# Four transposing transfers in place of TensorE transposes for one batch's residual, in an attention-and-mixing kernel

## The chip, the cores and the metric

The kernel runs on one core of one Trainium2 chip. The core has five engines that each work through their own instructions in order: TensorE (PE, matrix products; its weight loads are shown apart as PEld), VectorE (DVE), ScalarE (ACT), GpSimd (POOL) and SyncE (SP). SyncE computes nothing here: it issues transfers (DMAs), which sixteen transfer engines then carry out between the chip's memory and the core's own, or within the core's own. Engines wait for each other on semaphores. The metric is the device time of one execution in microseconds; a smaller time is better. Small differences are told by the median of several runs.

## The reference, cut to what matters

Eight batches, eight heads, 576 positions, 64 channels a head. An attention over means of four positions and an attention over a narrow band (positions less than 4 apart) are added; the result, 576 x 512 a batch, is x. A second stage mixes it:

```python
theta = x @ w_theta
zr, zi = x * cos(theta), x * sin(theta)
y = einsum('ts,bsd->btd', w_tok_r, zr) + einsum('ts,bsd->btd', w_tok_i, zi)
u = x + y
out = u + maximum(u @ w_ch, 0.0)
```

The change concerns the last line: u is needed twice, once as an operand of the product with w_ch (channels on the partitions) and once as the residual that is added to it (positions on the partitions). One of the two is a transpose of the other.

## The kernel before, in words

The work is cut into small steps, each a function with a two-letter name, called with a batch b and a number. One long hand-written list, ORDER, says in which order the steps are emitted. The loop at the end reads it word by word: the first two letters name the step, what follows names its place (a bank of the accumulator memory, a slot of the staging memory, or the engine: v, a, g for VectorE, ScalarE, GpSimd). The b and the number are not in the word; they come from the step's own list in STEPS, in turn. `pin()` chains every instruction to the one before on the same engine, so each engine, SyncE too, runs exactly in the order of ORDER. Semaphore waits between engines are put in by the framework where data or buffers demand them. Batches overlap: while one batch is mixed, the next two or three are loaded, turned and run through attention.

The steps that matter here, for one batch:

- **Loads.** `lk`, `lq` (L287, four each) bring k and q into one of 16 staging slots, 288 KB each; `lv`, `lw` (L347, five each) bring v, 128 KB each. `ck`, `cq` (L295) cast k and q to bfloat16 on the engine named, `cv` (L396) does so for v. SyncE issues the loads in the order of the list, ahead of their use.
- **Attention.** `tp` (L302) transposes k or q on TensorE, for half of the heads at a time; `ev` (L315) brings the result back. For batch 7 `dk` (L306) does so by transposing transfers instead, and `ev` copies at L312. `kd`, `qd` (L329 to L335, or one VectorE instruction) take the means of four, `sd` (L426) the coarse scores, `nd`, `xn` their use; `ps` (L482), `ex`, `mk` (L503, L505), `po` (L515), `nm` (L523, L524) are the banded attention, `xt` (L537) turns its result, and `xa` (L545) adds the coarse one, which gives x with channels on the partitions (tile xT).
- **Mixing.** `th` (L556), `cs` (L561, L562), `xm` (L595) and `zz` make z; the last 64 positions go through `tt`, `ct`, `zt` (L577) and, from batch 4, `dz` (L581), a transposing transfer that writes row block 8 of z. `mx(b, i)` (L636) is nine matmuls that sum over the row blocks 0 to 8 of z in turn, eight such groups a batch; `ua(b, i)` (L641, VectorE) adds xT and writes 288 positions of 128 channels of uT. Two steps, ua(b, 2c) and ua(b, 2c+1), complete channel block c.
- **Residual.** ur[b % 2] holds u with positions on the partitions. For the batches in RPE, `up(b, c)` (L650) makes four TensorE transposes of 128 x 128 into a bank and `uc(b, c)` (L653) copies them out, once for each 128 positions. For the other batches `du(b, c)` (L645) is one transposing transfer issued by SyncE, 128 channels x 512 positions, once for each 128 channels; it needs ua(b, 2c) and ua(b, 2c+1).
- **Output.** `ch(b, c)` (L666) is the product with w_ch for 128 positions, `rl(b, c)` (L674, VectorE) clips it and adds ur, `st` (L680) stores it. The last 64 positions of two batches go together: `ut`, `dt` (L695), `ht` (L700), `rt` (L704), `ss`, `sr` (L709).

RPE is (0, 1, 2, 3): batches 0 to 3 use up and uc, 4 to 7 use du. In the list, the eight steps of batch 3 stand in lines 86 to 88: up(3,0) and up(3,1) after rl(2,3), then uc(3,0) on VectorE and uc(3,1) on ScalarE, up(3,2) and uc(3,2) on ScalarE after mx(4,2), up(3,3) before ch(3,0) and uc(3,3) on ScalarE after rl(3,1). The steps ua(3,0) to ua(3,7), on which they depend, stand in lines 81 to 85, among the loads of batches 6 and 7 and the attention of batches 4 to 6.

Of the kernel before, what the change touches and what calls it, by code (L numbers as in the profile page):

```python
# [44 lines left out]

XDMA = (6, 7)

RPE = (0, 1, 2, 3)
ZPE = (0, 1, 2, 3)

QKD = (7,)
# [26 lines left out]
tp01 eva mx6 mkg xt45 xt23 ua ua cva cvg cvg xt01 cka ts cvg xa xa mx7 th6 xa po45 nm pv23 tt0 th1 lk4 xm4 st st mkg  # L78
th5 vdv st cs nd23 ua zz ct cqg cqg ztg tp67 th4 cs dt po01 cs cs te xn evv po23 mx5 kdg qdg xm4 xm6 mx7 nm ps01 ex nm
ps23 ua lvd ua ex ch5 ps01 ex qdg zz lw lw xm7 zz rl kdg zp6 zz mkg nd23 xn lv1 lva lv3 mx5 zca sd67 lw ps01 ex po34  # L80
mx2 ua lw ed tp01 sd67 cva nm po34 eva cvv cvg ed lw up5 uca ua mx2 cvg nm cvg lvc xd3 ua pv04 xcv lk7 lk0 mx7 lq9 lq6
lq2 lqd lq8 lqb lq5 ckg ckg vda lq7 lw xt56 mkv cqg cqg po34 lk4 xt01 xa xa ch2 st cva ts lv6 th5 up6 ckg xm0 nm th1
tp34 cs ucv cs mkg rl eva mx6 ua ua th1 xt67 lk0 lk1 cs cqa po45 mkv xa nm ht3 rt tp67 th1 eva zz xm2 lv9 xm3 xm4 lw
lve zz zz ckg dk4 kdv mx0 cqg tp67 nd23 xn cs zz ua cqa eva mx1 nd67 xn cqa sr cqa cka tt2 ct dkb up4 cva cva ua mx0
mx7 ua cvg cvv uca te po01 nm qdg kdg qdg sd56 ed po23 ua ch4 rl xd0 ch1 ztg lw nm up7 ch4 uca xca po23 dz xt67 rl evg
ckg nm st st pv15 vda mx0 ps23 xa ex rl up1 up7 evg ua ucv mx6 uca ss ps01 ex xt45 cqa utg xa ua lv1 dk4 ps23 ex mx7
up0 uca th4 lvb sd56 mkv po23 lw lw xt01 utg dt ua dk7 cvv nm th7 du ed ts evg nd56 xa nd23 tt0 xn xn ct qdg mkv mkg
evv mx1 ztg xd2 up0 ua cs ch3 rl cs te mx4 ch7 qdg ps56 rl xcv ua mx1 ex cvg po23 po45 ua uca ps67 ex ht1 nm nm st st
rt cva ss mx0 ua po67 xt45 nm ps23 st xa ex ts du kdg th1 xm0 xm7 cs th6 cs xm4 zz zz zz ch5 rl kdg mx7 ua th0 po67 nm
cs te xt45 xa sd12 ch3 xm0 ch7 ch4 xt56 st ed sd12 mkg mkg ed ts zz dz lw mx0 lv1 du du cvv lw cvg th1 cs rl uta mx3  # L90
st rl rl xa dxb ua po45 po67 pv02 nm nm ua du mx1 vda ch4 dx mkg ua po23 po01 po67 rl sr nm mx5 ua mx4 tt5 dx1 du nm
nm nd23 xn nd01 st mx6 th7 mx2 cs xn xd3 mx0 ua ua xcv ua ua xt67 utv ct dx st st xt45 xt23 xa ch1 rl th0 ch6 ch1 ch7
cs xa xa tt0 zz zz th2 th3 cs st du du ch4 rl zz zz ztg ct dz rl mx2 mx0 mx1 cs ua ua st dxe dx ht0 ua th1 cs th3 dx7
dx zz st st mx2 rl mx1 ua ua cs zz dt mx3 mx1 mx2 zz zz ztg dz mx7 ua mx3 du du du mx6 rt ua ua utg ua st rl du st mx7
mx4 ua ua ua sr mx7 mx6 mx5 ua ua ua du du ua ch7 ch6 ss ch5 rl rl ch7 ch6 ch4 ch3 du du st uta dt sta rl st rl ht7
ch2 sta rl st rl sta rl st rt ssa sr rl sta rm su k0
"""


# [1 line left out]
def kernel(  # L101
# [605 lines left out]
    def tail_store(e):  # L707
        def step(i, w):
            QUEUE.get(w, nc.sync).dma_start(out=out[2 * i + e, 512:576, :], in_=at["ot", i][HALF * e:HALF * e + HALF])  # L709
        return step  # L710
# [3 lines left out]
    def span(*ns):  # L714
        out = [()]
        for n in ns:
            out = [x + (i,) for x in out for i in range(n)]
        return out
# [14 lines left out]
        zp=(zp, [(b,) for b in ZPE]), zc=(zc, [(b,) for b in ZPE]),  # L733
        up=(up, [(b, c) for b in RPE for c in range(4)]), uc=(uc, [(b, c) for b in RPE for c in range(4)]),
        xm=(xm, [(b, c) for b, c in span(B, 4) if b not in XDMA]), dx=(dx, [(b, c) for b, c in span(B, 4) if b in XDMA]), zz=(zz, span(B, 4)), mx=(mx, span(B, 8)),
        ua=(ua, span(B, 8)), du=(du, [(b, c) for b, c in span(B, 4) if b not in RPE]), ut=(ut, span(B)), ch=(ch, span(B, 4)), rl=(rlf, span(B, 4)),
        st=(st, span(B, 4)), rm=(rm, [(B - 1, 3)]), su=(su, [(B - 1, 3)]), dt=(dt, span(4)), ht=(ht, span(4)), rt=(rt, span(4)), ss=(tail_store(0), span(4)), sr=(tail_store(1), span(4)),
# [70 lines left out]
```

## Time and profile before

| What | Value |
|---|---|
| median of three runs | 231.59 us (231.36 to 231.72) |
| profiled execution, whole time | 231.04 us |
| profiled execution, span from first to last instruction | 229.3 us |
| SyncE's transposing transfers ur<-uT | 16, median issue 1224 ns |
| TensorE transposes at L650 | 64, mean 219 ns each |
| copies at L653 | 9 on ScalarE (median 588 ns), 7 on VectorE (416 ns) |
| moved by transfers | 49.41 MB, mean 216 GB/s |

The profile describes one execution. Its page gives each engine's busy time; a line of digits, one for each fortieth of the span, shows the busy tenths. The chain of waits is followed back from the last instruction: each piece is what the next one waited for, so only time in this chain can be saved or lost directly. A timeline lists an engine's instructions in order of time: start, duration, engine, source line, operation, what is written and read, shapes, how many, and in brackets how long the engine had stood idle and what ended that. For SyncE the duration is that of issuing a transfer, not of the transfer itself; the transfer lands some microseconds later. Matmuls overlap in the array, so the mean of one is longer than its share of the time.

### The profile page before, as it was taken

What the parts mean: (1) busy time and instruction counts of PE and PEld (TensorE: products, weight loads), DVE (VectorE), ACT (ScalarE), POOL (GpSimd) and SP (SyncE); (2) the same over time, 40 slices, a digit from 0 to 9 for tenths busy, and PEclk for the clock granted to TensorE, in tenths of its full rate; (3) what the DMA queues carried; (4) which work ended last, traced back from release to release, by engine and by line L of the source; (5) the groups of instructions that cost most, each with busy time, mean ns of one, the idle gap of its engine ahead of it and who ended that gap; (6) DMA issues with size and microseconds to landing.
All of it is one profiled execution on the core that took longest, in us unless ns stands there. A gap on an engine that the chain in (4) does not pass through costs nothing.

```text
span 229.3 us, 9430 instructions
## 1 busy us (share of the span) xinstructions
PE 219.4 (96%) x3970; PEld 152.3 (66%) x3970; DVE 187.8 (82%) x370; ACT 154.3 (67%) x240; POOL 147.4 (64%) x194
## 2 busy tenths in 40 slices
PE   7997899999999999999999999989998999999992
PEld 2475678776878666885785685766655775667741
DVE  6599998989988899889978798798986967648473
ACT  2279999689988999898888997868786132530000
POOL 7589998879996999997978399379933020200000
PEclk9999999999999999999999999999999999999999
DMA  6999987999998799979799996992473466655787
GB/s 180 394 390 390 294 176 212 370 326 174 319 336 162 196 297 265 203 163 284 157 261 353 270 146 175 136 131 77 90 152 84 71 139 186 139 146 132 152 223 268
DMA packets 76795, 49.41 MB, mean 216 GB/s; under 512 B 61136, under 2 KB 61392, under 8 KB 76752
## 3 DMA queue, kind: packets, MB, share of 16 engines
q1 hardware_dynamic: 76096, 47.76, 80.7%
q10 hardware_dynamic: 656, 1.05, 1.3%
q8 instruction: 31, 0.51, 1.0%
q14 instruction: 12, 0.10, 0.2%
HBM read 33.98 MB, written 9.44 MB: 189 GB/s over the span
## 4 chain that ended last, share of the span: by engine, by line
PE 75%; DVE 10%; DMA 5%; POOL 4%; issue 2%; ACT 2%; SPq 0%; DVEq 0%; POOLq 0%; ACTq 0%
PE PS L636 27%; PE PS L666 10%; PE PS L556 10%; PE PS L302 5%; DMA ur<-uT 4%; PE PS L515 2%; PE PS L537 2%; PE PS L595 2%; PE PS L764 2%; PE PS L482 2%; PE PS L568 2%; POOL two L329 1%; POOL pm L503 1%; PE PS L447 1%; DVE pm L505 1%
## 5 line engine op out<-in xcount | busy, mean ns | idle before, releaser
L636 PE MATMUL PS<-WT,z 128*128 128x288 bf16 x576 | 78.1, 286 | 0.0
L636 PEld LDWEIGHTS <-z 128*128 128x128 bf16 x576 | 53.9, 98 | 16.1 <-issue 1.3
L641 DVE TENSOR_TENSOR uT<-PS,xT 128x288 bf16<-128x288 f32 x64 | 28.5, 451 | 10.2 <-PE PS L636 9.4
L561 ACT ACTIVATE cs<-PS,pihc 128x512 bf16<-128x512 f32 x32 | 22.1, 690 | 21.0 <-PE PS L556 13.4
L556 PE MATMUL PS<-wth,xT 128*128 128x512 bf16 x128 | 32.1, 379 | 0.1
L666 PE MATMUL PS<-wch,uT 128*128 128x512 bf16 (+1 forms) x132 | 31.1, 373 | 0.0
L524 DVE TENSOR_TENSOR tmp<-PS,rl 128x512 bf16<-128x512 f32 x40 | 27.6, 691 | 1.4
L545 DVE TENSOR_TENSOR xT<-PS,xdT 128x928 bf16<-128x928 f32 (+1 forms) x24 | 22.3, 952 | 3.7 <-PE PS L537 3.6
L490 ACT ACTIVATE pm<-PS 128x1024 bf16<-128x1024 f32 (+1 forms) x24 | 20.5, 880 | 6.6 <-PE PS L482 5.4
L674 DVE SCALAR_TENSOR_TENSOR osb<-PS,ur 128x512 f32<-128x512 f32 x28 | 19.1, 685 | 6.7 <-DMA ur<-uT 3.9
L577 POOL TENSOR_TENSOR zT<-xT,cst 128x512 bf16<-128x512 bf16 x7 | 10.0, 1422 | 21.8 <-ACT cst L574 21.8
L295 POOL CAST k_tm<-st 128x576 bf16<-128x576 f32 x23 | 15.5, 691 | 7.6 <-DMA st<-in_k_dram 7.5
L770 ACT ACT_TABLE_LOAD x15 | 19.2, 1283 | 0.3
L666 PEld LDWEIGHTS <-uT 128*128 128x128 bf16 x132 | 11.9, 98 | 11.2
L295 POOL CAST q_tm<-st 128x576 bf16<-128x576 f32 x24 | 17.0, 725 | 3.3 <-DMA st<-in_q_dram 3.2
L562 ACT ACTIVATE cs<-PS 128x512 bf16<-128x512 f32 x32 | 19.1, 598 | 0.0
L396 POOL CAST v_w<-st 128x512 bf16<-128x512 f32 x21 | 13.4, 656 | 8.5 <-DMA st<-in_v_dram 8.5
L556 PEld LDWEIGHTS <-xT 128*128 128x128 bf16 x128 | 11.4, 98 | 10.3 <-DVE xT L545 0.7
L503 POOL TENSOR_TENSOR pm<-pm,band 128x512 bf16<-128x512 bf16 x16 | 18.1, 1158 | 0.0
L329 POOL TENSOR_TENSOR two<-qT 128x576 f32<-128x576 bf16 x14 | 16.5, 1177 | 1.5 <-ACT qT L315 1.2
L620 DVE TENSOR_TENSOR z<-PS,cs 128x1024 bf16<-128x1024 bf16 x24 | 15.8, 683 | 0.8 <-issue 0.4
L329 POOL TENSOR_TENSOR two<-kT 128x580 f32<-128x580 bf16 x13 | 15.0, 1154 | 0.4
(123 smaller groups left out, 421.5 us busy)
## 6 DMA issues: line engine op xcount, KB each, us to landing
st<-in_k_dram SPq DMA_DIRECT2D x32, 288.0 KB, 6.2
st<-in_q_dram SPq DMA_DIRECT2D x32, 288.0 KB, 5.8
st<-in_v_dram SPq DMA_DIRECT2D x70, 128.0 KB, 4.9
out_dram<-osb SPq DMA_DIRECT2D x26, 256.0 KB, 3.5
st<-in_v_dram SPq DMA_DIRECT2D x4, 288.0 KB, 3.0
st<-in_moe_w_tok_r_dram SPq DMA_DIRECT2D x4, 288.0 KB, 6.2
st<-in_moe_w_tok_i_dram SPq DMA_DIRECT2D x4, 288.0 KB, 6.0
st<-in_moe_w_theta_dram SPq DMA_DIRECT2D x4, 256.0 KB, 5.9
```

The lines of the kernel that those rows point to most:

```text
L295: COPY[w](out=to, in_=of)
L329: nc.gpsimd.tensor_tensor(out=t, in0=src[:, :, 0:2], in1=src[:, :, 2:4], op=ALU.add)
L490: nc.scalar.activation(out=pm[(3 * b + u) % NPM][:, :, 0:n].rearrange("p e c j w -> p e (c j w)"), in_=at.pop(("ps", b, u))[:, :, 0:4 * W ...
L503: EW[w].tensor_tensor(out=t[:, x], in0=t[:, x], in1=m[:, x], op=ALU.mult)
L524: nc.vector.tensor_tensor(out=tmp[(NCH * b + c) % NTMP].rearrange("p g (j d) -> p g j d", d=D), in0=ps[:, :, :, 0:D], in1=r.unsqueeze(3).t ...
L545: nc.vector.tensor_tensor(out=xT[b % 2][:, :, lo:lo + cnt].rearrange("p e (m j) -> p e m j", j=4), in0=at.pop(("xt", b, u))[:, :, 0:cnt].r ...
L556: nc.tensor.matmul(out=ps, lhsT=xT[b % 2][:, dc, P * c:P * c + P], rhs=wth[:, dc, :], start=(dc == 0), stop=(dc == 3))
L561: nc.scalar.activation(out=t[:, 0, :], in_=ps, func=AF.Sin, bias=pihc, scale=1.0)
L636: nc.tensor.matmul(out=ps, lhsT=z[b % 2][:, j, P * dc:P * dc + P], rhs=WT[:, j, cols], start=(j == 0), stop=(j == 8))
L641: nc.vector.tensor_tensor(out=uT[b % 2][:, dc, cols], in0=at.pop(("mx", b, i)), in1=xT[b % 2][:, dc, cols], op=ALU.add)
L666: nc.tensor.matmul(out=ps[:, cols], lhsT=uT[b % 2][:, dc, P * c:P * c + P], rhs=wch[:, dc, cols], start=(dc == 0), stop=(dc == 3))
L770: nc.scalar.activation(out=idle, in_=pihc, func=TABLE[kind])
```

## The change

Batch 3 leaves RPE. Its eight steps up and uc go out of the list, and four steps du come into it, one after each of ua(3,1), ua(3,3), ua(3,5) and ua(3,7). All other words keep their order, banks and slots. du(3,0) so stands after lv(6,3) and ahead of lk(6,3), lk(7,0) and the loads of q for batches 6 and 7; du(3,1) ahead of lk(7,2) and lk(7,3); du(3,2) between dk(7,0) of q and lw(7,0); du(3,3) ahead of lw(7,0) and dz(4). The functions are not changed. The lines of the list are broken anew, so the diff shows more lines than it alters; cut to those with a change:

```diff
-RPE = (0, 1, 2, 3)
+RPE = (0, 1, 2)
...
-mx2 ua lw ed tp01 sd67 cva nm po34 eva cvv cvg ed lw up5 uca ua mx2 cvg nm cvg lvc xd3 ua pv04 xcv lk7 lk0 mx7 lq9 lq6
+mx2 ua lw ed tp01 sd67 cva nm po34 eva cvv cvg ed lw up5 uca ua mx2 cvg nm cvg lvc xd3 ua du pv04 xcv lk7 lk0 mx7 lq9
...
-tp34 cs ucv cs mkg rl eva mx6 ua ua th1 xt67 lk0 lk1 cs cqa po45 mkv xa nm ht3 rt tp67 th1 eva zz xm2 lv9 xm3 xm4 lw
+th1 tp34 cs ucv cs mkg rl eva mx6 ua ua du th1 xt67 lk0 lk1 cs cqa po45 mkv xa nm ht3 rt tp67 th1 eva zz xm2 lv9 xm3
...
-lve zz zz ckg dk4 kdv mx0 cqg tp67 nd23 xn cs zz ua cqa eva mx1 nd67 xn cqa sr cqa cka tt2 ct dkb up4 cva cva ua mx0
-mx7 ua cvg cvv uca te po01 nm qdg kdg qdg sd56 ed po23 ua ch4 rl xd0 ch1 ztg lw nm up7 ch4 uca xca po23 dz xt67 rl evg
-ckg nm st st pv15 vda mx0 ps23 xa ex rl up1 up7 evg ua ucv mx6 uca ss ps01 ex xt45 cqa utg xa ua lv1 dk4 ps23 ex mx7
-up0 uca th4 lvb sd56 mkv po23 lw lw xt01 utg dt ua dk7 cvv nm th7 du ed ts evg nd56 xa nd23 tt0 xn xn ct qdg mkv mkg
-evv mx1 ztg xd2 up0 ua cs ch3 rl cs te mx4 ch7 qdg ps56 rl xcv ua mx1 ex cvg po23 po45 ua uca ps67 ex ht1 nm nm st st
+xm4 lw lve zz zz ckg dk4 kdv mx0 cqg tp67 nd23 xn cs zz ua cqa eva mx1 nd67 xn cqa sr cqa cka tt2 ct dkb up4 cva cva
+ua du mx0 mx7 ua cvg cvv uca te po01 nm qdg kdg qdg sd56 ed po23 ua du ch4 rl xd0 ch1 ztg lw nm up7 ch4 uca xca po23
+dz xt67 rl evg ckg nm st st pv15 vda mx0 ps23 xa ex rl evg ua mx6 ss ps01 ex xt45 cqa utg xa ua lv1 dk4 ps23 ex mx7
+th4 lvb sd56 mkv po23 lw lw xt01 utg dt ua dk7 cvv nm th7 du ed ts evg nd56 xa nd23 tt0 xn xn ct qdg mkv mkg evv mx1
+ztg xd2 ua cs ch3 rl cs te mx4 ch7 qdg ps56 rl xcv ua mx1 ex cvg po23 po45 ua ps67 ex ht1 nm nm st st rt cva ss mx0 ua
...
```

More of the change, by code (lines that the diff above doesn't have):

```diff
@@ L80 @@
 ps23 ua lvd ua ex ch5 ps01 ex qdg zz lw lw xm7 zz rl kdg zp6 zz mkg nd23 xn lv1 lva lv3 mx5 zca sd67 lw ps01 ex po34
-mx2 ua lw ed tp01 sd67 cva nm po34 eva cvv cvg ed lw up5 uca ua mx2 cvg nm cvg lvc xd3 ua pv04 xcv lk7 lk0 mx7 lq9 lq6
-lq2 lqd lq8 lqb lq5 ckg ckg vda lq7 lw xt56 mkv cqg cqg po34 lk4 xt01 xa xa ch2 st cva ts lv6 th5 up6 ckg xm0 nm th1
-tp34 cs ucv cs mkg rl eva mx6 ua ua th1 xt67 lk0 lk1 cs cqa po45 mkv xa nm ht3 rt tp67 th1 eva zz xm2 lv9 xm3 xm4 lw
-lve zz zz ckg dk4 kdv mx0 cqg tp67 nd23 xn cs zz ua cqa eva mx1 nd67 xn cqa sr cqa cka tt2 ct dkb up4 cva cva ua mx0
@@ L85 @@
-mx7 ua cvg cvv uca te po01 nm qdg kdg qdg sd56 ed po23 ua ch4 rl xd0 ch1 ztg lw nm up7 ch4 uca xca po23 dz xt67 rl evg
-ckg nm st st pv15 vda mx0 ps23 xa ex rl up1 up7 evg ua ucv mx6 uca ss ps01 ex xt45 cqa utg xa ua lv1 dk4 ps23 ex mx7
-up0 uca th4 lvb sd56 mkv po23 lw lw xt01 utg dt ua dk7 cvv nm th7 du ed ts evg nd56 xa nd23 tt0 xn xn ct qdg mkv mkg
-evv mx1 ztg xd2 up0 ua cs ch3 rl cs te mx4 ch7 qdg ps56 rl xcv ua mx1 ex cvg po23 po45 ua uca ps67 ex ht1 nm nm st st
-rt cva ss mx0 ua po67 xt45 nm ps23 st xa ex ts du kdg th1 xm0 xm7 cs th6 cs xm4 zz zz zz ch5 rl kdg mx7 ua th0 po67 nm
@@ L90 @@
[L90 to L94, printed above, removed]
@@ L95 @@
-mx4 ua ua ua sr mx7 mx6 mx5 ua ua ua du du ua ch7 ch6 ss ch5 rl rl ch7 ch6 ch4 ch3 du du st uta dt sta rl st rl ht7
-ch2 sta rl st rl sta rl st rt ssa sr rl sta rm su k0
+mx2 ua lw ed tp01 sd67 cva nm po34 eva cvv cvg ed lw up5 uca ua mx2 cvg nm cvg lvc xd3 ua du pv04 xcv lk7 lk0 mx7 lq9
+lq6 lq2 lqd lq8 lqb lq5 ckg ckg vda lq7 lw xt56 mkv cqg cqg po34 lk4 xt01 xa xa ch2 st cva ts lv6 th5 up6 ckg xm0 nm
+th1 tp34 cs ucv cs mkg rl eva mx6 ua ua du th1 xt67 lk0 lk1 cs cqa po45 mkv xa nm ht3 rt tp67 th1 eva zz xm2 lv9 xm3
@@ new lines @@
+po67 xt45 nm ps23 st xa ex ts du kdg th1 xm0 xm7 cs th6 cs xm4 zz zz zz ch5 rl kdg mx7 ua th0 po67 nm cs te xt45 xa
+sd12 ch3 xm0 ch7 ch4 xt56 st ed sd12 mkg mkg ed ts zz dz lw mx0 lv1 du du cvv lw cvg th1 cs rl uta mx3 st rl rl xa dxb
+ua po45 po67 pv02 nm nm ua du mx1 vda ch4 dx mkg ua po23 po01 po67 rl sr nm mx5 ua mx4 tt5 dx1 du nm nm nd23 xn nd01
+st mx6 th7 mx2 cs xn xd3 mx0 ua ua xcv ua ua xt67 utv ct dx st st xt45 xt23 xa ch1 rl th0 ch6 ch1 ch7 cs xa xa tt0 zz
+zz th2 th3 cs st du du ch4 rl zz zz ztg ct dz rl mx2 mx0 mx1 cs ua ua st dxe dx ht0 ua th1 cs th3 dx7 dx zz st st mx2
@@ L97 @@
+rl mx1 ua ua cs zz dt mx3 mx1 mx2 zz zz ztg dz mx7 ua mx3 du du du mx6 rt ua ua utg ua st rl du st mx7 mx4 ua ua ua sr
+mx7 mx6 mx5 ua ua ua du du ua ch7 ch6 ss ch5 rl rl ch7 ch6 ch4 ch3 du du st uta dt sta rl st rl ht7 ch2 sta rl st rl
+sta rl st rt ssa sr rl sta rm su k0
 """
```

## The prediction

> **What bounds the kernel now.** First the page: the span, the busy shares, the granted clock and the chain that ended last.
>
> ```profile
> span 229.3 us, 9430 instructions
> ...
> PE 219.4 (96%) x3970; PEld 152.3 (66%) x3970; DVE 187.8 (82%) x370; ACT 154.3 (67%) x240; POOL 147.4 (64%) x194
> ...
> PEclk9999999999999999999999999999999999999999
> ...
> GB/s 180 394 390 390 294 176 212 370 326 174 319 336 162 196 297 265 203 163 284 157 261 353 270 146 175 136 131 77 90 152 84 71 139 186 139 146 132 152 223 268
> ...
> PE 75%; DVE 10%; DMA 5%; POOL 4%; issue 2%; ACT 2%; SPq 0%; DVEq 0%; POOLq 0%; ACTq 0%
> ```
>
> TensorE is busy 96% of the span and carries 75% of the chain, at a granted clock of 1.0. Every stage but one is therefore priced in TensorE time, and a TensorE pause is paid in full unless a later wait takes it up. The exception shows when the chain of waits is asked for the stretch after 143 us:
>
> ```profile
> 144.94 0.55 PE PS L650 x8
> ...
> 147.51 1.12 DVE xT L545
> ...
> 148.92 1.75 DVE pm L505
> ...
> 156.67 0.69 DVE osb L674
> ...
> 170.44 4.34 DMA ur<-uT
> ```
>
> From 147.5 to 176 us it runs through VectorE, GpSimd and transfers; after that TensorE takes it again. Two of the four `up` steps that the change removes (L650 x8, 0.55 us) stand in this chain.
>
> Next I read SyncE's timeline, because the four new transfers go into its queue, which holds every load and most stores in program order:
>
> ```profile
> 114.92 2.26 SPq L287 DMA_DIRECT2D st<-in_k_dram  x2
> 117.23 4.17 SPq L287 DMA_DIRECT2D st<-in_q_dram  x8
> ...
> 123.00 0.62 SPq L287 DMA_DIRECT2D st<-in_k_dram  x1
> ...
> 138.41 1.22 SPq L581 DMA_TRANSPOSE z<-zT  x1
> ```
>
> Matched one by one with the words of ORDER, the row at 114.92 is lk(6,3) and lk(7,0) (the 28th and 29th load of k), 117.23 the eight lq of batches 6 and 7, then, left out here, lw(6,3), and 123.00 lk(7,1). The first new word, du(3,0), stands just ahead of lk(6,3), so SyncE will come to it at 114.9 us. It needs both additions of its 128 channels. VectorE's timeline has line 641 eight times a batch; these are the 26th, 28th and 32nd, that is ua(3,1), ua(3,3) and ua(3,7):
>
> ```profile
> 120.34 0.46 DVE L641 TENSOR_TENSOR uT<-PS,xT 128x288 bf16<-128x288 f32 x1 [0.52 <-PE PS L636]
> ...
> 127.81 0.46 DVE L641 TENSOR_TENSOR uT<-PS,xT 128x288 bf16<-128x288 f32 x1 [0.89 <-PE PS L636]
> ...
> 139.81 0.45 DVE L641 TENSOR_TENSOR uT<-PS,xT 128x288 bf16<-128x288 f32 x1
> ```
>
> So SyncE, which runs about 6 us ahead of VectorE here, would stand still from 114.9 until 120.8 with twelve loads behind it. Whether those have time to spare is read on GpSimd, which casts them, and on TensorE, which uses the casts:
>
> ```profile
> 119.79 0.67 POOL L295 CAST k_tm<-st 128x576 bf16<-128x576 f32 x1 [1.46 <-DMA st<-in_k_dram]
> 121.23 1.72 POOL L295 CAST q_tm<-st 128x576 bf16<-128x576 f32 x2 [0.77 <-DMA st<-in_q_dram]
> ...
> 129.63 0.66 POOL L295 CAST k_tm<-st 128x576 bf16<-128x576 f32 x1 [3.84 <-DMA st<-in_k_dram]
> 130.24 0.67 POOL L295 CAST q_tm<-st 128x576 bf16<-128x576 f32 x1
> ...
> 136.61 0.67 POOL L335 TENSOR_TENSOR qd<-two 128x288 bf16<-128x288 f32 x1
> ```
>
> ```profile
> 126.00 0.67 PE L302 MATMUL PS<-ident,q_tm 128*128 128x128 bf16 x9
> ...
> 132.96 0.67 PE L302 MATMUL PS<-ident,q_tm 128*128 128x128 bf16 x9
> ...
> 138.73 0.36 PE L426 MATMUL PS<-qd,kd 64*64 64x144 bf16 x12
> ```
>
> They have not. GpSimd already waits for lk(6,3) (1.46), lq(6,0) (0.77) and lk(7,1) (3.84). TensorE's room behind it: tp(6,0,1) at 126.00 against casts ending at 122.95, 3.05 us; tp(6,1,1) at 132.96 against 130.91, 2.05; sd(6,0) at 138.73 against the means ending at 137.28, 1.45. From 129.63 to that end GpSimd goes without a gap, so what delays lk(7,1) delays the means.
>
> **The change part by part.** *Added: four transposing transfers.* The same instruction stands in the trace sixteen times:
>
> ```profile
> L645 SPq DMA_TRANSPOSE ur<-uT x16: 1189/1224/1316, 150.9 to 218.1; - x16
> ...
> DMA to landing us min/median/max: 2.4/2.9/4.3
> ```
>
> Each costs SyncE 1.22 us and lands in 2.9. The landing hides: the reader rl(3,0) is the row at 156.67 above, and the last new transfer lands some ten us earlier. The order is what costs. du(3,0) issues at 120.85 and ends at 122.1, so lk(6,3) is issued at 122.1 in place of 114.92, 7.2 us late. When it lands comes from a load of the same size in an empty queue, and its followers from the rate that the transfers reached here:
>
> ```profile
> st<-in_v_dram SPq DMA_DIRECT2D x4, 288.0 KB, 3.0
> ```
>
> ```profile
> 122.00:126.00 4.00, 4.00 (x102) 2.31 (x101) 3.33 (x6) 3.35 (x6) 3.79 (x5) 1.00 1.05 380
> 126.00:130.00 4.00, 4.00 (x63) 2.60 (x62) 2.74 (x7) 3.58 (x7) 0.37 (x1) 1.00 1.10 274
> ```
>
> (The last two columns are DMA share and GB/s; the transfers are saturated in both.) Then: lk(6,3) lands at 122.1 + 3.0 = 125.1, against a cast at 119.79 before. lq(6,0), two loads of 0.295 MB on, at 380 GB/s: 126.65. Its two casts take 1.72, so they end at 128.37 and not 122.95; less 3.05 of room, **TensorE pauses 2.4 us** at tp(6,0,1). lk(7,1): nine loads at 380 GB/s (2.65 MB, 7.0 us), then lw(6,3) and itself at 274 (0.43 MB, 1.55 us): 133.65, or 4.0 later than 129.63. At tp(6,1,1) that is 4.0 - 2.05 = 1.95, inside the 2.4 already lost; at sd(6,0) it is 4.0 - 1.45 = 2.55, so TensorE is 2.55 late there. Bounds: the fastest slice of the page moves 394 GB/s, which gives 7.8 us for all 3.08 MB, 3.3 us late, no more than the 2.4 pause; the pace of before from 119.79 to 129.63, 9.84 us, gives 5.3 late and a pause of 3.85. I take 2.55, by the windows of this very stretch.
>
> du(3,1) comes to SyncE at about 130, ua(3,3) is done at 128.27 + 2.4 = 130.7: a short wait, and behind it lk(7,2), lk(7,3) and loads of v that are cast later still. du(3,2) comes between. du(3,3) waits for ua(3,7): 140.26 + 2.4 = 142.66, ends 143.9; behind it stand lw(7,0) and dz(4), which now issues at 144.7 in place of 138.41. It lands 2.4 later (row below), at 147.1. The ninth matmul of mx(4,0) needs it; the group starts at 143.28, its ninth at 144.36, with the 2.55 at 146.9: **0.2 more**.
>
> ```profile
> z<-zT SPq DMA_TRANSPOSE x4, 2.4
> ```
>
> ```profile
> 143.28 1.28 PE L636 MATMUL PS<-WT,z 128*128 128x288 bf16 x9
> ```
>
> SyncE's lag itself ends later, where it idles:
>
> ```profile
> 152.22 1.85 SPq L680 DMA_DIRECT2D out_dram<-osb  x2
> 162.64 0.55 SPq L709 DMA_DIRECT2D out_dram<-osb  x1
> ```
>
> Between 154.1 and 162.64 it waits for rt(1), which follows TensorE; an arrival 6 us later does no harm. From 162.64 it issues nearly without a break to the transfer that ends the chain's piece at 174.78, so TensorE's delay at rt(1) is passed on to the rest.
>
> *Removed: sixteen transposes on TensorE, one copy on VectorE, three on ScalarE.*
>
> ```profile
> L653 ACT COPY ur<-PS x9: 579/588/610, 50.2 to 159.6; 128x512 bf16<-128x512 bf16 x9
> L653 DVE COPY ur<-PS x7: 412/416/425, 56.4 to 145.6; 128x512 bf16<-128x512 bf16 x7
> ```
>
> ```profile
> 147.51 1.12 DVE L545 TENSOR_TENSOR xT<-PS,xdT 128x928 bf16<-128x928 f32 x1 [1.55 <-PE PS L537]
> ```
>
> up(3,0) and up(3,1) are the eight matmuls in the chain, 0.55 us; VectorE then waits for TensorE, so this is gained. up(3,3) stands just ahead of ch(3,0) on TensorE: half of 0.55, 0.28. up(3,2) is worth nothing, since it lies beside the mask multiplication on VectorE from 148.92 to 150.67, for which TensorE waits next. VectorE's 0.42 stands ahead of its 1.55 of idle time: nothing. ScalarE's 3 x 0.59 fall in a 67% busy engine that the chain doesn't touch there: nothing. Gain: **0.83 us**.
>
> [...] The rows have 0.55 us for eight pipelined ones, 0.07 each. [...]
>
> **Sum**: +2.55 + 0.2 - 0.83 = +1.92 us. The profiled execution took 231.04 us (its span of 229.3 and 1.74 around it); the sum makes it 232.96. The median of the three runs shown is 231.59, so the forecast is 233.5 us.
>
> **Rivals.**
> 1. *The queue recovers and the removed work wins.* The transfers are saturated, so a load waits in their queue; while SyncE stands, the queue drains, and later loads land sooner after issue. To beat the 0.83 gain, lq(6,0)'s casts must end under 3.9 us late (they come out at 5.4) and lk(7,1) under 2.3 (4.0). That would take 3.08 MB in under 6.8 us, 450 GB/s, where no slice exceeds 394, and a landing 1.5 us sooner than in an empty queue. If so: 231.59 - 0.83 = 230.8. 9%; some 5% more for ending within 0.46 us of before.
> 2. *A second wait.* Full queues stretch an issue: the transpose at 130 us of k_tm took 2.92 us against 1.22. If du(3,1) and du(3,3) do, and the loads keep the old pace, lk(7,1) is 5.3 us late: 3.25 at tp(6,1,1), 3.85 at sd(6,0). ua(3,7) then ends at 143.5, du(3,3) at 146.5, dz(4) issues at 147.2 and lands at 149.6, where the ninth matmul of mx(4,0) is due at 148.2, another 1.4. 3.85 + 1.4 - 0.83 = +4.4: 236.0. 16%.
>
> ```profile
> 130.32 2.92 SPq L306 DMA_TRANSPOSE st<-k_tm  x1
> ```
>
> 3. *The pause makes TensorE cold.* At its start six 512-column matmuls took 2.74 us, 0.46 each, against 0.97 for four in the middle. If a pause brought that back for a stretch as long as those six, half of 2.74 would be lost, 1.4 us: 234.9. Against it, the granted clock stays 1.0 throughout. 4%.
>
> ```profile
> 1.26 2.74 PE PS L226 x6
> ...
> 78.07 0.97 PE PS L556 x4
> ```
>
> [...]
>
> That the transfers aren't made, or the transposes stay, is excluded by the diff.
>
> **How the numbers follow.** Forecast 66% (its own range 232.7 to 235.3: 394 GB/s gives 2.4 - 0.83 = +1.6, the old pace 3.85 + 0.2 - 0.83 = +3.2, with half a us about them), rival 1 9% and no change 5%, rival 2 16%, rival 3 4%. About 0.2%, 0.46 us, is what a measurement of this kernel can tell from no change. The range goes from 232.4 to 236.3, with rival 2 in it and rival 1 outside. Faster 0.09, same 0.05, slower 0.86.
>
> **What would show it.** Right: SyncE's first new L645 row starts right after ua(3,1), near 120.9, with a gap of about 6 us before it; GpSimd's idle time before the cast of lk(6,3) grows from 1.46 to about 7; TensorE shows a pause of about 2.4 us before L302 near 126; L426 of batch 6 starts near 141.3; the tail from 177 us on is the old one, moved. Wrong: casts of batch 6 on time although the loads are issued late; a TensorE pause in another place; or SyncE coming to du(3,0) later than I read, so that nothing waits.

## The result, and the profile after

The changed kernel takes 240.06 us (median of six runs, 237.86 to 241.50) against 231.41 for the kernel before (six runs, 230.37 to 231.72): a ratio of 1.0358, 95% interval 1.0305 to 1.0411, so 7.1 to 9.5 us slower. The forecast was slower, but 233.5, and its range ended at 236.3. The sign was right; the size was a quarter of the measured one. The page below is of the slowest of the six runs (241.50 us), a slow execution that the ratio leaves out; a second profile of the same kernel, at 239.46 us, stands beside it further down.

First the page of the changed kernel:

```profile
span 239.8 us, 9370 instructions
...
PE 219.6 (92%) x3927; PEld 153.5 (64%) x3954; DVE 188.2 (79%) x369; ACT 152.9 (64%) x237; POOL 146.9 (61%) x194
...
PE   7896999999999999999993999689999899999992
...
PEclk9999799999999999999999799979999999999999
...
L636 PE MATMUL PS<-WT,z 128*128 128x288 bf16 x576 | 80.3, 291 | 2.2 <-DMA z<-zT 2.2
```

TensorE's busy time is what it was (219.6 us, 219.4 before), though sixteen of its matmuls are gone (the page has 43 matmul records fewer, but only sixteen weight loads, 3954 against 3970; the other 27 records are missing from the trace), and its share fell from 96 to 92%: it waits more and, in places, runs slower. The digits say where. A slice is 6.0 us: slice 22 (126 to 132 us) has a 3, slices 26 and 27 a 6 and an 8, where before a 9 stood. The clock's row, all nines before, dips at slices 23 and 27. (It also dips at slice 5, long before the first changed word; this execution reaches mx(3,0), the first matmul group of batch 3, at 118.1 us, against 116.6 before. In the profiled executions of this study that start lies anywhere from 116.4 to 118.8, with no difference between the kernels up to there that would explain it. So times are compared below as counted from the start of mx(3,0).)

SyncE's timeline of the changed kernel (start, time to issue, line, transfer) shows the wait that was foreseen:

```profile
111.97 4.00 SPq L347 DMA_DIRECT2D st<-in_v_dram  x4
122.33 1.22 SPq L645 DMA_TRANSPOSE ur<-uT  x1
123.60 1.04 SPq L287 DMA_DIRECT2D st<-in_k_dram  x2
124.69 2.33 SPq L287 DMA_DIRECT2D st<-in_q_dram  x5
```

Between 115.97 and 122.33 SyncE stands still, 6.4 us, and the loads of batches 6 and 7 come only after it. GpSimd's timeline shows what this does to the casts; the bracket is the time that it stood idle, and for what:

```profile
126.74 0.67 POOL L295 CAST k_tm<-st 128x576 bf16<-128x576 f32 x1 [6.90 <-DMA st<-in_k_dram]
128.58 0.67 POOL L295 CAST q_tm<-st 128x576 bf16<-128x576 f32 x1 [1.18 <-DMA st<-in_q_dram]
130.72 0.67 POOL L295 CAST q_tm<-st 128x576 bf16<-128x576 f32 x1 [1.47 <-DMA st<-in_q_dram]
...
136.78 0.67 POOL L295 CAST k_tm<-st 128x576 bf16<-128x576 f32 x1 [2.56 <-DMA st<-in_k_dram]
```

And TensorE's timeline, which pays for it:

```profile
126.65 1.03 PE L556 MATMUL PS<-wth,xT 128*128 128x512 bf16 x4
131.45 1.14 PE L302 MATMUL PS<-ident,q_tm 128*128 128x128 bf16 x9 [3.77 <-POOL q_tm L295]
...
145.69 0.36 PE L426 MATMUL PS<-qd,kd 64*64 64x144 bf16 x12
...
150.24 1.15 PE L636 MATMUL PS<-WT,z 128*128 128x288 bf16 x8
153.56 0.30 PE L636 MATMUL PS<-WT,z 128*128 128x288 bf16 x1 [2.16 <-DMA z<-zT]
```

There are two pauses: 3.77 us before tp(6,0,1), which waits for the second cast of q, and 2.16 us inside mx(4,0), whose ninth matmul waits for dz(4). The first nine transposes after the pause take 1.14 us where nine took 0.67 before. The windows of the same kernel say why (busy time of PE, PEld, DVE, ACT, POOL, then the granted clock, the DMA share and GB/s):

```profile
127.76:131.17 3.41, 0.00 (x0) 0.00 (x0) 0.68 (x2) 1.13 (x2) 1.12 (x2) 1.00 0.99 338
131.17:134.58 3.41, 3.13 (x19) 2.34 (x20) 0.00 (x0) 1.12 (x1) 3.05 (x4) 0.50 1.08 346
151.65:155.06 3.41, 1.50 (x41) 1.16 (x42) 1.04 (x2) 0.77 (x1) 0.00 (x0) 1.00 0.65 204
155.06:158.48 3.42, 3.42 (x91) 2.30 (x89) 1.32 (x2) 2.34 (x4) 0.66 (x1) 0.50 0.98 193
```

From 131.17, near the end of the first pause, and from 155.06, 1.5 us after the second, the clock is granted at half for 3.41 us. Between 131.17 and 134.58 TensorE is busy 3.13 us and gets 19 matmuls done.

What TensorE has lost at each landmark, counted from the start of mx(3,0) and against the same place in the kernel before (from the starts of the groups of L636 in the traces; the second profile of the changed kernel and two experiments of the next section stand beside it):

| up to the start of | changed | changed, second profile | only du(3,0) in place | only du(3,3) in place |
|---|---|---|---|---|
| mx(3,2) | 0.0 | 0.0 | 0.0 | 0.1 |
| mx(3,3), after the first pause | 4.4 | 4.5 | 4.8 | 0.1 |
| mx(3,4), after the halved clock | 5.5 | 5.7 | 6.2 | 0.1 |
| mx(4,0) | 5.5 | 5.7 | 6.2 | 0.7 |
| mx(4,1), after the second pause | 7.3 | 6.6 | 5.7 | 2.1 |
| mx(4,3) | 8.4 | 5.8 | 5.3 | 2.4 |
| mx(5,0) | 8.1 | 6.6 | 5.0 | 2.2 |
| mx(6,0) | 8.8 | 5.6 | 4.1 | 1.3 |
| end of the span | 9.0 | 6.8 | 4.7 | 1.8 |

Of the 9.0 us, 8.4 are lost between 126 and 164 us; from mx(5,0) on the rest is the old one, moved, within a us. The second profile has the first pause (3.87 us) and the halved clock after it as well, but its second pause is shorter, and the clock stays at 1.0 behind it (1.00 from 151.0 to 154.4 us; the nine matmuls of L636 at 155.46 take 1.28):

```profile
152.84 0.30 PE L636 MATMUL PS<-WT,z 128*128 128x288 bf16 x1 [1.15 <-DMA z<-zT]
```

So the second halving is not in every execution. This one loses 6.8 us from mx(3,0) on; its whole time is 8.4 us above that of the profiled execution of before, and the other 1.6 lie ahead of mx(3,0), where the two kernels do the same.

### The profile page after: what moved, and what is told of

Its sections match the earlier page's. It is cut to its first block, busy times and chain, and to the rows that moved or that the text cites. A ratio compares the mean times of both kernels' runs of the same rounds, so it can differ in the third digit from the quotient of the medians.

```text
span 239.8 us, 9370 instructions
## 1 busy us (share of the span) xinstructions
PE 219.6 (92%) x3927; PEld 153.5 (64%) x3954; DVE 188.2 (79%) x369; ACT 152.9 (64%) x237; POOL 146.9 (61%) x194
## 5 line engine op out<-in xcount | busy, mean ns | idle before, releaser
L636 PE MATMUL PS<-WT,z 128*128 128x288 bf16 x576 | 80.3, 291 | 2.2 <-DMA z<-zT 2.2
L636 PEld LDWEIGHTS <-z 128*128 128x128 bf16 x576 | 54.8, 99 | 19.3 <-DMA z<-zT 2.5
L556 PE MATMUL PS<-wth,xT 128*128 128x512 bf16 x116 | 31.1, 384 | 0.7 <-issue 0.2
L666 PE MATMUL PS<-wch,uT 128*128 128x512 bf16 (+1 forms) x122 | 29.8, 372 | 1.0 <-issue 0.6
L295 POOL CAST k_tm<-st 128x576 bf16<-128x576 f32 x23 | 16.0, 708 | 11.6 <-DMA st<-in_k_dram 11.5
L556 PEld LDWEIGHTS <-xT 128*128 128x128 bf16 x128 | 11.8, 100 | 10.5 <-issue 0.5
L295 POOL CAST q_tm<-st 128x576 bf16<-128x576 f32 x24 | 16.3, 694 | 3.5 <-DMA st<-in_q_dram 3.5
```

The source lines that it names most:

```text
L295: COPY[w](out=to, in_=of)
L556: nc.tensor.matmul(out=ps, lhsT=xT[b % 2][:, dc, P * c:P * c + P], rhs=wth[:, dc, :], start=(dc == 0), stop=(dc == 3))
L636: nc.tensor.matmul(out=ps, lhsT=z[b % 2][:, j, P * dc:P * dc + P], rhs=WT[:, j, cols], start=(j == 0), stop=(j == 8))
L666: nc.tensor.matmul(out=ps[:, cols], lhsT=uT[b % 2][:, dc, P * c:P * c + P], rhs=wch[:, dc, cols], start=(dc == 0), stop=(dc == 3))
```

## The experiments

Ratios are to the kernel before, run on the same chip. The words are those of ORDER; where du moves, the list of du in STEPS is put in the new order of issue.

### Is it the wait, or the transfers?

**Only the wait.** The kernel before, batch 3's transposes still on TensorE, with one transposing transfer of 128 x 128 into an unused tile at the place of du(3,0):

```diff
-lvc xd3 ua pv04 xcv lk7
+lvc xd3 ua wy pv04 xcv lk7
...
+    def wy(b, w):
+        nc.sync.dma_start_transpose(out=scr, in_=uT[b % 2][:, 0, 384:512])
```

A first form read positions 0 to 127 in place of 384 to 511. Those are written by ua(3,0) alone, so it waits for the addition before the one that du(3,0) waits for, and is a milder case than the change.

> The kernel before with its TensorE transposes, and one small transposing transfer (128 x 128, into a tile that nothing reads) at the place of du(3,0), which waits for ua(3,1) as du(3,0) does. Theory: SyncE stands still for about 6 us and the loads behind it are as late as in the changed kernel, so TensorE pauses 3 to 4 us before L302 near 126 and the clock is halved once; 5 to 6 us slower than before, 236 to 238 us. Rival (the transfers' own work): a quarter of one of four transfers, under 0.5 us, so 231 to 232.

> The kernel before with its TensorE transposes, and one small transposing transfer (128 x 128, into a tile that nothing reads) at the place of du(3,0). It reads positions 384 to 511, which ua(3,1) writes, where the first such run read positions 0 to 127, which ua(3,0) completes 2.1 us earlier. Theory (the loss goes with the time that SyncE stands still): SyncE stands 2 us longer than in the first such run, TensorE pauses 3 to 4 us before L302 near 126 in place of 1.25, and the clock may be halved for 3.4 us; 4 to 6.5 us slower than before. Rival (the transfers' own work, or the number of transfers): the same 2.5 us as the first such run or less.

The first form issued at 118.52, TensorE paused 1.25 and 0.94 us, and the granted clock was 1.00 from 124.0 to 130.8 us: 234.37 us, ratio 1.0126 (1.0035 to 1.0217). The second form, by SyncE's and TensorE's timelines:

```profile
110.65 4.01 SPq L347 DMA_DIRECT2D st<-in_v_dram  x4
121.45 1.15 SPq L650 DMA_TRANSPOSE scr<-uT  x1
```

```profile
130.55 0.99 PE L302 MATMUL PS<-ident,q_tm 128*128 128x128 bf16 x9 [3.76 <-POOL q_tm L295]
```

SyncE stands still for 6.8 us, TensorE pauses for 3.76, and behind the pause it runs at half its pace: the nine matmuls of L636 at 131.33 take 2.37 us, the nine at 138.07 take 1.27. 236.12 us, ratio 1.0186 (1.0144 to 1.0228). One small transfer that nobody reads, with nothing removed and nothing else added, costs 4.3 us: the wait ahead of the loads is enough.

**Only the transfers.** The kernel before with four transposing transfers of full size at the change's four places, which read u of batch 2, long complete, and write ur[1] before anything of use stands there:

```diff
+    def wy(dc, w):
+        nc.sync.dma_start_transpose(out=ur[1][:, :, P * dc:P * dc + P], in_=uT[0][:, dc, 0:512])
```

> The kernel before with its TensorE transposes, and four transposing transfers of full size at the places of the change that read the finished u of batch 2 and write the residual tile before its copies overwrite it, so that nothing has to be waited for. Theory: each costs SyncE 1.2 us of issue and the transfer engines 0.6 us; lk(6,3) is 1.2 us late against 3 us of room: 231.2 to 233 us, no pause over 1 us, clock 1.0. Rival (the transfers' own work): the loss of the change in full, 238 us or more.

SyncE's timeline, and TensorE's at the place of the pause:

```profile
112.00 4.12 SPq L347 DMA_DIRECT2D st<-in_v_dram  x6
116.61 1.23 SPq L648 DMA_TRANSPOSE ur<-uT  x1
117.89 1.50 SPq L287 DMA_DIRECT2D st<-in_k_dram  x2
```

```profile
128.25 0.67 PE L302 MATMUL PS<-ident,q_tm 128*128 128x128 bf16 x9
```

The transfer goes out 0.5 us after the loads ahead of it, and TensorE has no pause there: 232.95 us, ratio 1.0028 (0.9989 to 1.0066). The four transfers in the same queue, which did not have to wait, cost at most 0.7%.

**The change, later.** All four du behind dk(7,1) of q:

```diff
-ua dk7 cvv nm
+ua dk7 du du du du cvv nm
```

> All four new transfers stand together after dk(7,1,1), ahead of du(4,0), instead of each right after its additions; nothing else differs from the changed kernel. Theory (the place in SyncE's queue costs, because a transfer that waits holds up the loads behind it): no load of batch 6 or 7 is late, TensorE has no pause before L302 near 126 us and the granted clock stays 1.0; the last transfer lands near 158.5, so rl(3,0) on VectorE waits 1 to 2 us; time 230.6 to 232.8 us. Rival (the transposing transfers themselves cost, as work of the transfer engines): the same four are made, so 237 us or more. Rival (the clock falls at random in the changed kernel): 237 or more in most runs.

231.93 us, ratio 1.0037 (0.9996 to 1.0078), and no pause in TensorE near 126 (the same row stands at 126.82 with no bracket). The transfers now land last at 159.1 us, and VectorE, which adds the residual, waits for it:

```profile
159.22 1.29 DVE L674 SCALAR_TENSOR_TENSOR osb<-PS,ur 128x512 f32<-128x512 f32 x2 [1.80 <-PE PS L482]
```

(The bracket names the last event by the profile, PE's; that had long been done. The transfers' landing at 159.09 is what fits.)

### Which of the four?

One or two stay in the change's place, the others go behind dk(7,1):

```diff
-lvc xd3 ua du pv04
+lvc xd3 ua pv04
...
-ua dk7 cvv nm
+ua dk7 du du cvv nm
```

(The removals differ by experiment, one word for each du that leaves its place.) Only the first stays:

> du(3,0) at its place in the change, the other three together after dk(7,1,1). Theory: the first wait makes the greater part, a pause of 3.5 to 4 us and often a halved clock (1.5 us), less 0.8 for the removed transposes: 4 to 6 us slower than before; dz(4) is not held by du(3,3), so there is no second pause over 0.5 us in mx(4,0). Rival (each of the four transfers costs about the same): 2 us slower than before.

236.30 us, ratio 1.0188 (1.0142 to 1.0234); a pause of 4.32 before tp(6,0,1), the clock halved after it (0.57 on the mean of 131 to 135 us), and no pause in mx(4,0). The same kernel in a later comparison, below: 1.0228 (1.0182 to 1.0273). Only the last stays:

> du(3,3) at its place in the change, ahead of lw(7,0) and dz(4), the other three together after dk(7,1,1). Theory: dz(4) is issued after ua(3,7), near 141.5, and lands near 144.5 us, when the ninth matmul of mx(4,0) is due at 144.4: a pause under 0.7 us there and no halved clock; within 1 us of the kernel with all four late, 231 to 233 us. Rival (the second pause comes from du(3,3) alone): a pause of 2 us in mx(4,0) as in the changed kernel, 234 us or more.

233.74 us, ratio 1.0103 (1.0048 to 1.0158): not what my theory said, which had the wait of du(3,3) nearly free. Only the two in the middle stay:

> du(3,1) and du(3,2) at their places in the change, du(3,0) and du(3,3) together after dk(7,1,1). Theory (a transfer costs by what it holds up): du(3,1) waits from 125 to 128.3 us ahead of lk(7,2) and lk(7,3), which have 3 to 4 us of room, so the loss over the kernel with all four late is under 1 us: 1.003 to 1.008 of before. Rival (these two make up the part of the loss that first and last alone leave open, 2 to 3 us): 1.013 or more.

230.83 us, ratio 0.9985 (0.9960 to 1.0009): no loss, where I had expected 0.3 to 0.8%. Behind du(3,1) and du(3,2) stands nothing that is scarce. First and last stay:

> du(3,0) and du(3,3) at their places in the change, du(3,1) and du(3,2) together after dk(7,1,1). Theory (two pauses and two halved clocks make the loss): about as slow as the whole change, 1.028 to 1.037 of before, with a second halved clock near 155 us in most runs. Rival (the two middle transfers carry the rest): the sum of first alone and last alone, 1.025 or less.

238.61 us, ratio 1.0281 (1.0224 to 1.0339), with pauses of 3.58 and 2.10 us. First and last alone give 1.9 to 2.3% and 1.0%, the pair 2.8%, the whole 3.6%: within their intervals, the loss is that of two places.

**Why the last one costs.** TensorE's timeline with only du(3,3) in place:

```profile
144.07 1.15 PE L636 MATMUL PS<-WT,z 128*128 128x288 bf16 x8
146.89 0.30 PE L636 MATMUL PS<-WT,z 128*128 128x288 bf16 x1 [1.67 <-DMA z<-zT]
```

and SyncE's:

```profile
140.60 1.19 SPq L645 DMA_TRANSPOSE ur<-uT  x1
141.84 0.62 SPq L347 DMA_DIRECT2D st<-in_v_dram  x1
142.57 1.24 SPq L581 DMA_TRANSPOSE z<-zT  x1
```

dz(4) is issued 4.2 us later than before (138.41) and the ninth matmul waits for it. To see whether that is all, du(3,3) was moved behind dz(4), and nothing else:

```diff
-po23 ua du ch4 rl
+po23 ua ch4 rl
...
-dz xt67 rl evg
+dz du xt67 rl evg
```

> As e7_last_only (only du(3,3) near its place, the three others late), but du(3,3) stands behind lw(7,0) and dz(4) instead of ahead of them. Theory (du(3,3) costs through dz(4), which waits behind it): dz(4) is issued by 139.5 as before and lands by 142, no pause at the ninth matmul of mx(4,0), ratio 0.997 to 1.002 against the 1.010 of e7. Rival (what cost in e7 was the three late transfers or the transposing transfer itself): ratio 1.006 or more although dz(4) is on time.

```profile
139.59 1.21 SPq L581 DMA_TRANSPOSE z<-zT  x1
140.89 1.22 SPq L645 DMA_TRANSPOSE ur<-uT  x1
```

```profile
143.82 1.28 PE L636 MATMUL PS<-WT,z 128*128 128x288 bf16 x9
```

The nine matmuls run without a break: 231.68 us, ratio 0.9979 (0.9937 to 1.0021) against the 1.0103. With du(3,3) behind lw(7,0) and dz(4) instead of ahead of them, the last transfer's price is gone; the two intervals don't overlap.

### The halved clock

`wm` emits matmuls of constants into a free bank (L764 in these kernels). Here it fills the pauses, so that TensorE doesn't rest:

```diff
-th1 tp34 cs ucv
+th1 wm3h0 tp34 cs ucv
...
-vda mx0 ps23
+vda wm0a0 mx0 ps23
```

Both in the whole change, then the first one alone:

> The changed kernel with 17 matmuls of 512 columns ahead of tp(6,0,1) and 10 ahead of mx(4,0), on a tile of zeros into banks that are overwritten right after, so that TensorE works in its two pauses. Theory (the pauses halve the clock for 3.4 us each, which costs about 2 us on top of the pauses): the granted clock stays 1.0 around 131 and 155 us and the kernel takes 236.5 to 238.5 us, 1.5 to 3 us less than the changed kernel; the loads are late as there. Rival (the pauses alone make the loss): no gain, or slower by the added matmuls, 240 to 242.

> The changed kernel with the 17 matmuls ahead of tp(6,0,1) alone, and none ahead of mx(4,0). Theory: the first halved clock is gone (1.5 us); the second pause of about 2 us stays and its halved clock comes in some runs: 1.025 to 1.032 of before. Rival (the second pause exists only because the first halved the clock): 1.020 or less.

238.02 us, 1.0274 (1.0195 to 1.0354), and 236.08, 1.0216 (1.0145 to 1.0286), the second a little less than expected. The clock stays at 1.0: in the first it is 1.00 from 127 to 135 us, and in both the nine matmuls of L636 right behind tp(6,0,1) take 1.27 us, where they took 2.36 in the second profile of the changed kernel. The loads come as late as without (lk(6,3) is cast at 126.64 in the first, at 126.74 in the changed kernel). What of this is the clock shows only against the unfilled kernel on the same chip:

> The changed kernel again, beside the one with work in the first pause. 1.030 to 1.041 of before; two halved clocks in most profiles.

> The changed kernel with 17 matmuls in the first pause. If the first halved clock adds to the end: 1.2 us or more faster than its partner although the second pause stays, and that in runs with the transfer of dz(4) as late as there. If only the second pause and its own halved clock count: within 0.6 us of its partner where dz(4) is as late, and faster only where dz(4) lands early.

239.44 us, 1.0359 (1.0312 to 1.0405), against 237.01, 1.0246 (1.0191 to 1.0301): 2.4 us less with the pause filled. (The profile of the unfilled kernel is the second one of the result; between 124 and 190 us it has one halved clock, where I had expected two.) And where only du(3,0) is in place:

> The kernel with du(3,0) alone at its place in the change, plus 17 matmuls of 512 columns on a tile of zeros ahead of tp(6,0,1), so that TensorE works through the pause. Theory (the halved clock is a cost of its own, half of 3.4 us, beside the pause): the pause's wall time stays, the clock stays 1.0, and the kernel takes 1.2 to 1.8 us less than without the matmuls, 1.011 to 1.014 of before. Rival (the halved clock falls where TensorE waits anyway): 1.017 to 1.021, as without the matmuls.

> du(3,0) alone at its place, timed beside the same kernel with work in the pause. If the halved clock adds to the end: 1.2 to 1.7 us slower than its partner. If it falls into later waits for late loads: within 0.6 us of its partner. Either way 1.014 to 1.023 of before.

> The same with 17 matmuls in the pause, clock 1.0. If the halved clock adds to the end: 1.008 to 1.014 of before. If it falls into later waits: as its partner, 1.015 to 1.023, with waits of TensorE for late data after 138 us that its partner has not.

236.81, 1.0228 (1.0189 to 1.0266) with the filling, so the lower time that my theory expected didn't come; and in one comparison 236.59, 1.0228 (1.0182 to 1.0273) without and 236.92, 1.0197 (1.0135 to 1.0259) with it. Here the full clock is worth nothing that can be told. It works, by the windows of 131 to 135 us, without and with the filling:

```profile
131.00:135.00 4.00, 4.00 (x22) 2.54 (x22) 0.79 (x2) 1.12 (x1) 2.73 (x3) 0.57 1.03 300
```

```profile
131.00:135.00 4.00, 4.00 (x63) 2.60 (x64) 2.24 (x5) 2.52 (x4) 2.69 (x3) 1.00 1.08 306
```

63 matmuls in place of 22 in the same four microseconds. But the loads behind are as late as before, and TensorE, earlier, waits for them further on:

```profile
130.91 0.68 PE L302 MATMUL PS<-ident,q_tm 128*128 128x128 bf16 x9 [0.64 <-POOL q_tm L295]
...
138.35 0.68 PE L302 MATMUL PS<-ident,q_tm 128*128 128x128 bf16 x9 [0.31 <-POOL q_tm L295]
...
144.71 0.26 PE L426 MATMUL PS<-qd,kd 64*64 64x144 bf16 x4 [0.27 <-POOL qd L335]
```

Why the filling gains 2.4 us in the whole change and nothing here stays open. A piece of it may lie at dz(4): with the filling, the pause in mx(4,0), which waits for it, was 0.59 us against 1.15. But from mx(3,0) on the two profiled executions differ by 0.5 us only.

### Is there a place that wins?

Two more placements, made to hold up nothing:

```diff
-sr cqa cka tt2
+sr du cqa cka tt2
...
-ztg lw nm up7
+ztg lw du nm up7
...
-ua dk7 cvv nm
+ua dk7 du du cvv nm
```

> The four transfers where SyncE stood idle and nothing urgent is queued behind: du(3,0) after sr(0) (1.5 us of idle time before dk(7,0,1)), du(3,1) after lw(7,0) (1.1 us before dz(4)), du(3,2) and du(3,3) after dk(7,1,1). Theory: no load is late and the last lands near 156, before rl(3,0) wants it at 156.7, so the removed TensorE transposes count: 0.3 to 0.9 us faster than before, 0.996 to 0.9985. Rival (transfers cost by contention wherever they stand): no gain, 1.000 to 1.005.

231.25 us, ratio 0.9988 (0.9951 to 1.0025). And with the two middle ones in the change's place, du(3,0) behind sr(0), du(3,3) behind dk(7,1):

> The four new transfers where nothing scarce waits behind them: du(3,1) and du(3,2) at the change's places, du(3,0) after sr(0), du(3,3) after dk(7,1) of q. Theory (the removed transposes are worth 0.3 to 0.8 us once no load is held up): ratio 0.9965 to 0.999, no pause before L302 near 126 nor in mx(4,0). Rival (the removed work lay beside other limits and is worth nothing): ratio 0.9995 to 1.003.

231.73 us, ratio 1.0012 (0.9975 to 1.0048); its profiled execution has a pause in mx(4,0) that I hadn't expected:

```profile
146.36 0.30 PE L636 MATMUL PS<-WT,z 128*128 128x288 bf16 x1 [1.22 <-DMA z<-zT]
```

du(3,0) and du(3,2) now stand ahead of dz(4), issued at 141.75. No version was faster than the kernel before by more than its interval.

## Why the prediction was wrong in size

**The wait and its place: right.** Counted from mx(3,0), du(3,0) was foreseen at 4.25 us (120.85 less 116.6) and came at 4.24; lk(6,3) was foreseen to land at 8.5 and its cast began at 8.65. SyncE's lag ended where it was foreseen, at rt(1): before its store at 172.30 SyncE stood idle for 9.1 us.

**"TensorE pauses 2.4 us" at tp(6,0,1): the mis-sized term.** It rests on "lq(6,0), two loads of 0.295 MB on, at 380 GB/s: 126.65", and on both casts following that landing without a break. In the profile after, lq(6,0) is cast at 10.5 (10.05 foreseen), but lq(6,1) only 2.14 us later, and it is the second cast that tp(6,0,1) needs. It ended at 13.3 and not 11.8. TensorE came to L302 3.95 us later than before, where 2.4 was foreseen.

The rate is not what failed. At 380 GB/s a load takes 0.78 us; by the transfer records the loads from lk(6,3) on landed 0.82, 1.03, 2.14, 0.73 and 0.74 us apart. One gap, the one between lq(6,0) and lq(6,1), holds nearly all of the 1.5 us that the term was short. What lay beside it is in the last section; its cause stays open.

The prediction's other bound, "the pace of before", comes near the measured pause by luck. Its 3.85 is 5.3 less the 1.45 of room at sd(6,0), though the text calls it a pause; at tp(6,0,1), with 3.05 of room, that pace gives 2.3. For lk(7,1) it was the better row: the cast came 5.65 late, where it says 5.3 and the forecast 4.0.

**"2.55 late" at sd(6,0): overtaken.** TensorE was 5.5 us late there, so the late means cost nothing of their own.

**"0.2 more" at mx(4,0): the second failed term.** The pause was 2.16 us and cost 1.9. Counted from mx(3,0), dz(4) was issued 9.3 us later than before with TensorE 5.5 late at mx(4,0); foreseen were 6.3 and 2.55. The distance between the two, 3.8 against 3.7, was right. What made the pause was the landing: 4.31 us after the issue, where "lands 2.4 later" had been taken from the four rows of before. Those 1.9 us, and the 0.1 of the distance, are what the pause has beyond the 0.2. In the second profile the pause was 1.15.

**"The pause makes TensorE cold", 4%: it happened.** The price per stretch, 1.4 us, was about right: TensorE was 3.95 late at L302 and 5.5 at mx(3,4), when the halved stretch was over. The argument against it, that "the granted clock stays 1.0 throughout", came from a trace that had no pause of that length; it said nothing about one. In the runs, each of the five pauses of 3.58 to 4.32 us in the last section was met by a lower clock, the pause of 2.16 us was followed by one, and one of 2.10 us was not. None of the pauses named there lies between 2.16 and 3.58 us, so what the foreseen one of 2.4 would have done isn't shown.

**"Gain: 0.83 us": not found.** Four placements that hold up little gave 0.9979 to 1.0012; the narrowest, the middle pair, says a gain of 0.3 us with an interval from 0.9 to a loss of 0.2. So 0.83 isn't excluded, nor is nothing.

**The rivals were priced one by one.** The second wait (236.0), the cold clock (+1.4) and the slower pace are no alternatives: behind the pause of 3.77 us the clock was at 0.50, and both push ua(3,7) and with it dz(4). The prediction's own prices for the three together, 3.85 + 1.4 + 1.4 - 0.83 = 5.8, make 237.4, near the lowest run of the changed kernel and 2.7 below its median. The range left that out. The second wait came another way than the rival had it: no issue was stretched (the four transfers took SyncE 1.19 to 1.31 us each), dz(4) was issued late and landed late. That full queues had made the 2.92 us of k_tm was my reading of that row; no run shows the cause.

## What to carry to other kernels

The transfer that had to wait was paid by the loads behind it in its queue (one small one cost 4.3 us, four that did not wait at most 0.7%): ask first what stands behind a transfer, and how much time that has to spare; here the place of one word was worth 1%. A rate gives the mean of a row of loads, but the next step waits for the landing of one, and here that one came 1.4 us behind the pace of its neighbours. And a pause whose size is uncertain should be priced both with and without a halved clock behind it (here 1.55 us: TensorE was 3.95 late at L302 and 5.5 at mx(3,4)), with the rivals that bring each other about added up and not weighed singly.

## What the runs showed of the hardware

**The clock.** Five profiled pauses of TensorE ahead of tp(6,0,1) were long, and each was met by a lower clock. (Where the clock is a mean of a window, the window stands with it.)

| kernel | pause, end | granted clock |
|---|---|---|
| the whole change | 3.77, 131.45 | 0.50 from 131.17 to 134.58 |
| the whole change, again | 3.87, 131.60 | 1.00 in 128.2 to 131.6, 0.50 in 131.6 to 135.0 |
| only du(3,0) in place | 4.32, 130.95 | 1.00 in 127 to 131, 0.57 in 131 to 135 |
| first and last | 3.58, 130.00 | 0.50 in 129.1 to 132.5 and in 132.5 to 135.93 |
| second form of the small transfer | 3.76, 130.55 | no window; nine matmuls of L636 take 2.37 us at 131.33, 1.27 at 138.07 |

Behind shorter pauses the clock stayed up: 1.25 us in the first form (1.00 from 124.0 to 130.8), 1.15 in the second profile of the change (1.00 from 151.0 to 154.4), 1.67 with only du(3,3) in place (1.00 from 143.0 to 149.8), 1.22 in the last placement (nines in the page's row of the clock up to its last slice). Of two near 2.1, the one of 2.16 in the changed kernel was followed by 0.50 from 155.06 to 158.48; behind the one of 2.10 in the kernel with first and last, nine matmuls of L636 took 1.28 us.

In the page of the changed kernel the three halved stretches begin at 25.36, 131.17 and 155.06 us and last 3.41 us each. In the 3.41 us ahead of them TensorE was busy for 2.10, 0.00 and 1.50 us. In the kernel with first and last it was busy for 1.30 of the 3.40 us from 150.0 to 153.4, and no lower clock followed. The stretch at 25.36 follows no pause of 0.9 us or more, so neither the length of a pause nor this busy time parts the cases, and what sets the clock isn't shown. With the pause filled it was 1.00 in place of 0.57 from 131 to 135 us where only du(3,0) is in place.

**A transfer that lands late.** dz(4), always the same transfer, landed 2.4 to 2.7 us after its issue in five of the profiles below; in the other three it took 4.3 us or more, as the record or the matmul that waits for it tells. The late ones have in their stretch a packet of the queue that the view names `q8 instruction` (16 KB, 0.88 to 1.76 us long in the traces of before and after); the others have none.

| kernel | view from, to | packets of q8 in it | dz(4) landed after |
|---|---|---|---|
| before | 136, 142 | none | 2.43 |
| all late | 139.2, 141.7 | none | 2.4 |
| the two in the middle | 136, 144 | none | 2.7 |
| du(3,3) behind dz(4) | 139.5, 143.9 | none | 2.4 |
| two other places (0.9988) | 141.6, 144.1 | none | 2.5 |
| the whole change | 149.2, 153.5 | one | 4.31 |
| only du(3,3) in place | 142.5, 147 | one | its matmul came 4.32 after the issue |
| last placement (1.0012) | 141.7, 146.4 | one | its matmul came 4.61 after the issue |

(The last two views also have one packet of 0.01 MB of the queue q14.) The view of the transfers from 149.2 to 153.5 us in the changed kernel, and that from 141.6 to 144.1 in the kernel of the fifth row (the last number is the time to landing):

```profile
q8 instruction: 1, 0.02, 1.6%
...
z<-zT SPq DMA_TRANSPOSE x1, 4.3
```

```profile
z<-zT SPq DMA_TRANSPOSE x1, 2.5
```

The traces of before and after have thirty transposing transfers of L581 and L645 whose landing is recorded. The ten with the start of a q8 packet between issue and landing took 3.06 to 4.34 us, the twenty without 2.42 to 2.74, but for one of 3.50. In one of the ten, of 3.43, the packet began only 0.03 us ahead of the landing.

The long gap ahead of lq(6,1) looks alike. Such a packet ran from 128.18 to 129.14, within it:

```profile
q8 instruction: 1, 0.02, 2.4%
```

(This is the view of the transfers from 127.5 to 130 us.) In the eight profiles with du(3,0), or the second form of the small transfer, ahead of lk(6,3) whose transfers were viewed from 122 to 131 us, the one q8 packet there fell between 126 and 129, after the cast of lk(6,3) had begun, and the second cast of q ended 4.5 to 5.2 us after that. Before the change it ended 3.16 us after, and a q8 packet had begun 0.62 us ahead of the landing of lq(6,1); with all four late it ended 2.90 after. With the first form of the small transfer it took 3.91, its packet in the window from 127 to 128, in which that cast ended, and with the four transfers that did not wait 4.35; the transfers of that one were not viewed there. All this is correlation: nothing was run that moves such a packet alone.
